# New task lists for a hand-scheduled recurrent-gate and soft-mixture kernel, with one small load moved to another queue

## Chip, cores and metric

One NeuronCore of a Trainium2 chip runs the whole kernel. The metric is the device time of one execution in microseconds (us), the median of several runs.

## What is computed

The reference, cut to what matters (float32 throughout, 4 sequences of 5056 tokens of 256 channels, 20224 tokens in all):

```python
# part 1: gated linear recurrence over time, for each channel
sig_r, sig_i = 1/(1+exp(-r_gate)), 1/(1+exp(-i_gate))
a_t  = exp(8 * sig_r * log(sigmoid(a_param)))
h    = a_t[:, t] * h + sqrt(1 - a_t[:, t]**2) * sig_i[:, t] * x[:, t]   # y[:, t] = h
# part 2: soft mixture of experts over all tokens y; phi is 256 x 32, 8 experts of 4 slots
logits = y @ phi
d = softmax(logits, over tokens);  slot_input = d.T @ y
slot_out = relu(slot_input[e] @ w1[e]) @ w2[e]          # 1024 hidden, for each expert e
out = softmax(logits, over slots) @ slot_out
```

## The kernel before

The tokens are cut into 40 blocks of 512 (the last has 256), called quads, and the quads into 22 units: unit 0 is quad 0, units 1 to 18 are pairs of quads, units 19 to 21 single ones. For each unit three loads come from HBM: `Dr` (the r gate, with channels on partitions), `Di` and `Dx` (the i gate and x, with tokens on partitions). A pair's load is 1 MiB. All of them go out on SyncE's queue; `w10` to `w27` are the 16 loads of expert weights, 1 MiB each, on the same queue (`w22` is the second matrix of expert 2).

What a unit goes through, with the names that the lists use (p is a unit, q a quad, h one of two halves of the channels, g a group of up to two units):

- ScalarE: `SRp` and `SIp` (a tanh each, lines 814 and 832), `EXp.h` (the exponential that makes a, line 888, for two units at once where they are paired), `RTp` (the square root, line 904). Exponential and tanh share one table of functions, the square root needs another, so roots are done in blocks between two table loads.
- `SQp.h` (a squared, line 873) on GpSimd or VectorE, now and then ScalarE.
- `Uq` (gated x) on VectorE or GpSimd. A string `IV` with one letter for each quad says how: D is one fused VectorE instruction (line 852); P is an addition of 1 on GpSimd (`P1q`, line 842) and a product (line 854); E is the product alone, and TensorE adds x to it by transposing two tiles into the same PSUM bank instead of one.
- TensorE: `TUp.h` (line 921) transposes gated x to channels on partitions, in PSUM. VectorE: `STp.h` (line 944) multiplies by the root, `SCp.h` (line 964) is the scan over time.
- `TYq` (line 987) transposes the result back, `YCq` (line 1001 or 1003) copies it out. `LGg`, `LEg`, `LDg`, `TEg`, `ESg`, `DMg`, `ACg`, `AEg` are the logits of a group (line 1047, reading `phi_sb`), their running maximum, and the softmax sum over tokens that is rescaled as it goes (`AE`, line 1135).

After the last unit comes a serial stretch: `W`, `SP`, `SL`, `SM` (merging four partial sums, lines 1327 to 1339), the expert layers `L1` and `L2`, and then the outputs: `CT`, `CM`, `CS`, `CE`, `RR`, `RC`, `CN` (softmax over slots), `OT` (line 1584), `OE` (lines 1599 and 1601) and the stores `OD` on SyncE's queue.

The order of work is not left to the hardware. `ORDER` has one list for each engine, written out task by task, and a list `B` in which the tasks that claim tiles from the shared pool `all_s` (48 slots of 512 KiB) must claim them. A planner in the same file (`Planner.run`) walks the lists with assumed durations to decide which slot each task gets, and emits the instructions in that order; each engine then runs its list from top to bottom, each instruction waiting for its inputs. The constants `XFER`, `LAG0` and the like are the planner's assumed transfer times; they act on the kernel through the slots that are given out.

Around the change: the kernel's constants are set up in `e_const` (which also starts the load of `a_param` on ScalarE's queue), `phi` is loaded on SyncE's queue right behind `Dx4` (line 756), and every logit task waits for that.

Of the kernel before, what the change touches and what calls it, by code (L numbers as in the profile page):

```python
# [15 lines left out]
P = 128  # L16
# [12 lines left out]
IV = 'DDDPEEEEDEEEEEEEEEEEEEEEEDDEEPEPPPPPPPPP'  # L29
# [42 lines left out]
PHI = 4  # L72
# [31 lines left out]
    ),  # L104
    "ACT": (
# [12 lines left out]
    ),  # L118
# [14 lines left out]
    ),  # L133
    "POOL": (
# [6 lines left out]
    ),  # L141
# [6 lines left out]
    ),  # L148
# [9 lines left out]
    ),  # L158
}
SWITCH = 0.09  # L160
WARMF = 1.4
COLD = 5.6
COLDX = 1.9
IDLE = 2.2
CHILL = 5.0
LOAD = 1.41

# [7 lines left out]
SI2 = ()  # L175
RT2 = ()
XFER = 1.265
ISSUE = 0.4
FIRST = 0.7
REACH = 2.6  # L180
REACHO = 1.55
LATO = 1.75
DEEP = 8
PEX = 1.03

ODS = 0

LAG1 = 0.8
LAG0 = 1.6

OUT2 = (4, 5, 6, 7, 8)

KIND = {
    "exp": ("exp", "ln"), "ln": ("ln",), "tanh": ("exp", "sig"), "sig": ("sig",), "sqrt": ("sqrt",),
}

class Task:
# [367 lines left out]
def kernel(  # L569
# [171 lines left out]
    def load(nm, p):  # L741
# [20 lines left out]
        if (nm, p) in (("r", 0), ("x", PHI)):  # L762
            ld[(nm, p)].parts = 2
# [935 lines left out]
```

## Time and profile before

| | |
|---|---|
| median of 3 runs | 285.18 us (285.14 to 285.29) |
| the profiled execution | 285.39 us |
| its span (first to last instruction on the core) | 283.6 us |
| granted TensorE clock, mean over the span | 0.994 |
| VectorE busy | 226.9 us of the span |
| ScalarE busy | 242.0 us |
| TensorE busy (identity transposes that fill gaps are counted) | 259.8 us |
| GpSimd busy | 184.8 us |
| moved by DMA | 100.07 MB |

An engine's busy time counts its instructions, not its waits for others; a VectorE or GpSimd instruction that is held up while it runs counts as busy. The span is what the timeline's zero and end refer to. The 1.8 us between the span and the execution's time lie outside the program's instructions.

### The profile page before, as it was taken

What the parts mean: (1) busy time and instruction counts of PE and PEld (TensorE: products, weight loads), DVE (VectorE), ACT (ScalarE), POOL (GpSimd) and SP (SyncE); (2) the same over time, 40 slices, a digit from 0 to 9 for tenths busy, and PEclk for the clock granted to TensorE, in tenths of its full rate; (3) what the DMA queues carried; (4) which work ended last, traced back from release to release, by engine and by line L of the source; (5) the groups of instructions that cost most, each with busy time, mean ns of one, the idle gap of its engine ahead of it and who ended that gap; (6) DMA issues with size and microseconds to landing.
All of it is one profiled execution on the core that took longest, in us unless ns stands there. A gap on an engine that the chain in (4) does not pass through costs nothing.

```text
span 283.6 us, 6612 instructions
## 1 busy us (share of the span) xinstructions
PE 259.8 (92%) x2760; PEld 208.2 (73%) x2760; DVE 226.9 (80%) x270; ACT 242.0 (85%) x247; POOL 184.8 (65%) x147
## 2 busy tenths in 40 slices
PE   7999798599989898898998899899999999999897
PEld 7999797469966676676677567565656677788796
DVE  0153999999999999998999989999974768758340
ACT  7898999999999999999999899999861279876620
POOL 4228769999999989996989999998110501211100
PEclk9999999989999999999999999999999999999999
DMA  7999999999999999995999998978850049999995
GB/s 229 422 425 424 419 416 419 424 422 417 422 419 381 383 407 415 424 387 202 419 374 391 344 410 316 340 249 317 326 232 2 2 192 414 418 424 421 423 416 226
DMA packets 14960, 100.07 MB, mean 353 GB/s; under 512 B 1745, under 2 KB 2002, under 8 KB 4306
## 3 DMA queue, kind: packets, MB, share of 16 engines
q1 hardware_dynamic: 14928, 99.65, 87.5%
q8 instruction: 21, 0.34, 0.5%
q14 instruction: 9, 0.07, 0.1%
q10 hardware_dynamic: 2, 0.00, 0.0%
HBM read 78.94 MB, written 20.71 MB: 351 GB/s over the span
## 4 chain that ended last, share of the span: by engine, by line
DVE 41%; PE 36%; DMA 11%; issue 7%; ACT 4%; POOLq 0%; SPq 0%; DVEq 0%; ACTq 0%
DVE all_s L964 19%; DVE pair L944 12%; DMA all_s<-in_i_gate_dram 8%; PE bank L1260 6%; PE bank L1584 5%; PE pair L921 4%; PE one L1260 3%; DVE yn L1003 3%; DMA all_s<-in_x_dram 3%; PE pair L987 3%; DVE all_s L852 2%; PE bank L1434 2%; PE bank L1382 2%; PE one L1047 2%; PE bank L1554 2%
## 5 line engine op out<-in xcount | busy, mean ns | idle before, releaser
L964 DVE TENSOR_TENSOR_SCAN all_s<-all_s,pair 128x1024 f32<-128x1024 f32 (+8 forms) x50 | 92.9, 1879 | 0.6
L854 POOL TENSOR_TENSOR all_s<-all_s 128x1024 f32<-128x1024 f32 (+1 forms) x34 | 79.9, 2370 | 6.9 <-ACT all_s L832 3.7
L873 POOL TENSOR_TENSOR all_s<-all_s 128x1024 f32<-128x1024 f32 (+2 forms) x40 | 70.7, 1795 | 17.6 <-ACT all_s L888 14.6
L921 PE MATMUL pair<-ident,all_s 128*128 128x128 f32 x480 | 59.0, 274 | 5.6 <-DVE all_s L964 4.0
L921 PEld LDWEIGHTS pair<-ident,all_s 128*128 128x128 f32 x480 | 52.6, 140 | 11.3 <-DVE all_s L964 4.4
L1260 PE MATMUL one<-ident 128*128 128x128 f32 x394 | 50.4, 282 | 0.5 <-DVE all_s L1061 0.5
L987 PE MATMUL pair<-ident,all_s 128*128 128x128 f32 x316 | 42.7, 280 | 7.3 <-DVE all_s L964 4.2
L1260 PEld LDWEIGHTS one<-ident 128*128 128x128 f32 x394 | 46.2, 146 | 1.5 <-DVE all_s L1061 0.7
L987 PEld LDWEIGHTS pair<-ident,all_s 128*128 128x128 f32 x316 | 34.9, 142 | 15.8 <-DVE all_s L964 6.4
L944 DVE SCALAR_TENSOR_TENSOR pair<-all_s,pair 128x1024 f32<-128x1024 f32 (+1 forms) x38 | 44.6, 1186 | 0.6 <-ACT all_s L904 0.2
L888 ACT ACTIVATE all_s<-all_s,ca 128x2048 f32<-128x2048 f32 (+3 forms) x28 | 43.9, 1589 | 0.1
L1531 POOL TENSOR_TENSOR all_s<-all_s,rs_all 128x512 f32<-128x512 f32 (+3 forms) x12 | 10.5, 897 | 48.8 <-DVE rs_all L1528 47.0
L832 ACT ACTIVATE all_s<-all_s 128x2048 f32<-128x2048 f32 (+2 forms) x22 | 38.1, 1731 | 2.2 <-DMA all_s<-in_i_gate_dram 2.2
L814 ACT ACTIVATE all_s<-all_s 128x2048 f32<-128x2048 f32 (+2 forms) x22 | 37.6, 1731 | 0.7 <-DMA all_s<-in_r_gate_dram 0.7
L904 ACT ACTIVATE all_s<-all_s 128x2048 f32<-128x2048 f32 (+2 forms) x22 | 37.2, 1733 | 0.1
L1001 ACT COPY yn<-pair 128x1024 f32<-128x1024 f32 (+1 forms) x25 | 24.4, 987 | 0.3 <-ACT yn L1001 0.3
L1047 PE MATMUL one<-all_s,phi_sb 128*32 128x256 f32 (+1 forms) x344 | 23.6, 382 | 0.5 <-DVE all_s L964 0.5
L1599 ACT COPY all_s<-bank 128x512 f32<-128x512 f32 (+1 forms) x38 | 20.0, 578 | 4.7 <-PE bank L1584 2.9
L1120 PE MATMUL one<-yn,eS 128*32 128x257 f32 x312 | 21.7, 386 | 2.4 <-ACT eS L1101 0.9
L1260 PE MATMUL bank<-ident 128*128 128x128 f32 x166 | 22.7, 275 | 0.8 <-ACT all_s L1599 0.7
L1601 DVE COPY all_s<-bank 128x512 f32<-128x512 f32 (+1 forms) x28 | 16.1, 604 | 6.8 <-PE one L1584 5.0
L1260 PEld LDWEIGHTS bank<-ident 128*128 128x128 f32 x166 | 18.6, 140 | 2.8 <-ACT all_s L1599 1.8
(115 smaller groups left out, 314.4 us busy)
## 6 DMA issues: line engine op xcount, KB each, us to landing
all_s<-in_r_gate_dram SPq DMA_DIRECT2D x18, 1024.0 KB, 10.8
all_s<-in_i_gate_dram SPq DMA_DIRECT2D x18, 1024.0 KB, 12.0
all_s<-in_x_dram SPq DMA_DIRECT2D x18, 1024.0 KB, 10.4
all_s<-in_moe_w_dram SPq DMA_DIRECT2D x16, 1024.0 KB, 7.6
out_dram<-all_s SPq DMA_DIRECT2D x5, 2048.0 KB, 9.8
out_dram<-all_s SPq DMA_DIRECT2D x8, 1024.0 KB, 6.7
all_s<-in_i_gate_dram SPq DMA_DIRECT2D x3, 512.0 KB, 4.4
all_s<-in_x_dram SPq DMA_DIRECT2D x3, 512.0 KB, 7.4
```

The source lines that it names most:

```text
L814: nc.scalar.activation(v, v, AF.Tanh, scale=0.5)
L832: nc.scalar.activation(v, v, AF.Tanh, scale=0.5)
L854: eng.tensor_tensor(out=o, in0=a, in1=b, op=ALU.mult)
L873: eng.tensor_tensor(out=t(Nb[(p, h)])[:, :c], in0=v, in1=v, op=ALU.mult)
L888: nc.scalar.activation(v, v, AF.Exp, scale=ca[:, h : h + 1], bias=ca[:, h : h + 1])
L904: nc.scalar.activation(v, v, AF.Sqrt, bias=f, scale=-f)
L921: nc.tensor.matmul(t(up)[:, i, m * P : (m + 1) * P], raw(nm, q)[:, m * D + h * P : m * D + (h + 1) * P], ident, is_transpose=True, start=( ...
L944: nc.vector.scalar_tensor_tensor(v, w, 1e-3 if gate_of(quads(p)[0]) == "S" else 0.5e-3, u, op0=ALU.max, op1=ALU.mult)
L964: nc.vector.tensor_tensor_scan(dst, dst, flat()[:, s0:s1], init, op0=ALU.mult, op1=ALU.add)
L987: nc.tensor.transpose(out=flat()[:, b * D + h * P : b * D + (h + 1) * P], in_=t(A[p])[:, h, i * QT + (b0 + b) * P : i * QT + (b0 + b + 1) ...
L1047: nc.tensor.matmul(o.rearrange("s (i p) -> s i p", p=P), phi_sb[:, h, :], t(A[p])[:, h, : plen(p)].rearrange("c (i j p) -> c j i p", j=nb, ...
L1260: nc.tensor.transpose(out=t(b)[:, 0, :P] if b.tag == "pair" else t(b)[:, :P], in_=ident, identity=ident)
```

## The change

Six things, all in one edit:

1. New lists in `ORDER`. VectorE's and ScalarE's tasks up to the merge differ in order, and four squares (`SQ0.0 SQ0.1 SQ1.0 SQ1.1`) go from GpSimd to VectorE, one (`SQ19.0`) from ScalarE to GpSimd. Loads and claims are in a new order. Among the tasks of the output stretch some 55 change between VectorE and ScalarE. `const2` (16 small copies on GpSimd) is put behind `U4`, `CE3` moves from the output stretch to a place ahead of `SR21`.
2. `IV`: quads 3, 29, 31 and 33 go from P to E, quads 28 and 30 from E to P.
3. `phi` is loaded from `e_const`, second on ScalarE's queue; it is gone from SyncE's queue, and the logits' tasks have no dependency on `Dx4` any more.
4. The planner takes 1.1 times the transfer time for loads of the first units.
5. `LAG0` is 0.1 instead of 1.6, for a first large load issued before 2.5 us.
6. `PHI` is gone, with what hung on it.

The heads of the lists (before, then after) and the rest of the diff:

```diff
-IV = 'DDDPEEEEDEEEEEEEEEEEEEEEEDDEEPEPPPPPPPPP'
+IV = 'DDDEEEEEDEEEEEEEEEEEEEEEEDDEPEPEPEPPPPPP'
-PHI = 4
     "DVE": (
-        "CA SQ3.1 U0 SQ3.0 SQ2.1 U1 U2 ST0.0 ST0.1 SC0.0 SC0.1 ST1.1 ST1.0 SC1.0 SC1.1 ST2.0 SC2.0 ST2.1 SC2.1 U8 YC0.0 "
+        "CA SQ0.0 SQ3.1 SQ0.1 SQ3.0 U0 SQ1.1 SQ2.1 SQ1.0 U1 U2 ST0.1 SC0.1 ST0.0 SC0.0 ST1.0 SC1.0 ST1.1 SC1.1 ST2.0 "
...
-        "SC20.1 LE9 LD9 LE10 ST21.1 LD10 SC21.1 ST21.0 SC21.0 MP AE9 LE11 LD11 MX AE10 W AE11 AF SL SM CM9 CS9 RR1 RR9 "
+        "SC20.0 SC19.1 ST20.1 AE8 SC20.1 LE9 ST21.1 LD9 LE10 LD10 SC21.1 ST21.0 SC21.0 MP AE9 LE11 LD11 MX W AE10 AE11 "
+        "AF CM10 SL CM9 SM RR3 CS10 CS9 RR1 RR9 CM5 HS0 CS5 RR10 RC3 RD HR0 CM0 RB1 CS0 RR5 RC9 RR0 RC0 HR1 SO RB5 RC10 "
     "ACT": (
-        "SA LN SI0 SR0 EX0.1 EX0.0 SR3 EX3.1 SR2 EX3.0 SR1 EX1.1 EX1.0 SI2 SI1 RT0.0 RT1.0 RT3.0 RT2.0 SI3 SR4 SR5 SI4 "
+        "SA LN SR0 SI0 EX0.1 EX0.0 SR3 EX3.1 EX3.0 SR2 SR1 EX1.1 EX1.0 SI1 SI2 RT0.0 RT1.0 RT3.0 RT2.0 SI3 SR4 SR5 SI4 "
     "PE": (
-        "CB TU0.0 TU0.1 TU1.1 TU1.0 TU2.0 TU2.1 TU3.1 LG0.0 LG0.1 LG0.2 TY0.0 TU3.0 LG1.0 TY2.0 TY1.0 TY3.0 LG1.1 LG0.3 "
+        "CB TU0.1 TU0.0 TU1.0 TU1.1 TU2.0 TU2.1 TY2.0 TU3.0 TY1.0 LG0.0 LG1.0 TY3.0 LG1.1 TU3.1 LG0.1 LG0.2 TU4.1 TY0.0 "
     "POOL": (
-        "const const2 SQ0.1 SQ0.0 SQ1.1 SQ1.0 SQ2.0 U4 P13 U3 U6 U5 U7 SQ5.0 SQ5.1 SQ4.0 SQ4.1 SQ6.0 SQ7.0 SQ7.1 U9 "
+        "const U3 SQ2.0 U4 const2 U6 U5 U7 SQ5.0 SQ4.1 SQ5.1 SQ4.0 SQ6.1 U9 SQ7.1 SQ7.0 SQ6.0 U10 U11 U12 LD0 U13 U14 "
     "SP": (
-        "Di0 Dr0 Dr3 Dr2 Dr1 Dx0 Di2 Dx1 Di1 Dx2 Dr4 Di3 Dr5 Dx3 Di4 Dx4 Dr7 Dr6 Di5 Di6 Dr9 Dx5 Dx6 Dr8 Di8 Dx7 Di7 "
-        "Dr11 Di9 Dx8 Dr10 Dr14 Dr15 Di10 Dx11 Dx9 Dr13 Dr12 Di11 Dx10 Di12 Dx12 w27 Di14 Dx14 Di13 Di16 w17 w13 Dx13 "
+        "Dr0 Di0 Dr3 Dr2 Dr1 Dx0 Di1 Di2 Dx1 Dx2 Dr5 Di3 Dr4 Dx3 Di4 Dx4 Dr7 Dr6 Di5 Dx5 Di6 Dx6 Di8 Dr9 Di7 Dr8 Dx7 Dx8 "
+        "Dr10 w22 Dr11 Di10 Di9 Di14 Dx9 Dx12 Dr12 Dx10 Dr13 Di11 Dx11 Di12 Di19 Dr14 Dr15 Dx14 Di13 w16 Di16 Dx13 Dx16 "
...
-LAG0 = 1.6
+LAG0 = 0.1
...
-                    landed[0] += LAG1 + (LAG0 if now < 1.9 else 0.0)
+                    landed[0] += LAG1 + (LAG0 if now < 2.5 else 0.0)
...
         nc.scalar.dma_start(out=row, in_=a_param.rearrange("(o c) -> o c", o=1))
+        nc.scalar.dma_start(out=phi_sb, in_=phi.rearrange("(p h) s -> p h s", p=P))
...
-            if (nm, p) == ("x", PHI):
-                nc.sync.dma_start(out=phi_sb, in_=phi.rearrange("(p h) s -> p h s", p=P))
...
-        ld[(nm, p)] = add("SP", f"D{nm}{p}", XFER * c / QT - (0.045 if c > QT else 0.5 if len(ld) == 0 else 0) + (0.27 if (nm, p) == ("x", PHI) else 0),
+        ld[(nm, p)] = add("SP", f"D{nm}{p}", XFER * c / QT * (1.1 if p < 4 - (nm != "r") else 1.0) - (0.045 if c > QT else 0.5 if len(ld) == 0 else 0),
...
-        if (nm, p) in (("r", 0), ("x", PHI)):
+        if (nm, p) == ("r", 0):
             ld[(nm, p)].parts = 2
...
-                         deps=[SC[(p, h2)] for h2 in range(h + 1)] + [ld[("x", PHI)]], gate=begun(lg),
+                         deps=[SC[(p, h2)] for h2 in range(h + 1)], gate=begun(lg),
```

## Rows read from the trace of the kernel before

**Rows 1.** The page: busy us (share of the span) xinstructions; DMA share, 40 slices, tenths.

```profile
PE 259.8 (92%) x2760; PEld 208.2 (73%) x2760; DVE 226.9 (80%) x270; ACT 242.0 (85%) x247; POOL 184.8 (65%) x147
...
DMA  7999999999999999995999998978850049999995
```

**Rows 2.** Windows: PE, PEld, DVE, ACT, POOL busy; PE clock, DMA share, GB/s.

```profile
20.00:30.00 10.00, 10.00 (x94) 10.00 (x93) 4.33 (x3) 8.79 (x6) 9.15 (x5) 1.00 1.01 422
30.00:40.00 10.00, 8.55 (x78) 8.17 (x77) 9.96 (x9) 9.97 (x7) 6.86 (x4) 1.00 1.02 417
...
150.00:160.00 10.00, 8.52 (x86) 6.99 (x79) 10.00 (x9) 9.01 (x11) 10.00 (x6) 1.00 0.96 376
160.00:170.00 10.00, 8.73 (x102) 5.74 (x103) 8.96 (x10) 9.95 (x8) 9.26 (x6) 1.00 0.97 392
```

**Rows 3.** Timeline of ScalarE: start, us, what [idle before it, and releaser].

```profile
24.18 1.92 ACT L832 ACTIVATE all_s<-all_s 128x2048 f32<-128x2048 f32 x1 [1.18 <-DMA all_s<-in_i_gate_dram]
26.11 1.28 ACT L904 ACT_TABLE_LOAD   x1
27.40 6.46 ACT L904 ACTIVATE all_s<-all_s 128x1024 f32<-128x1024 f32 x4
...
106.39 1.89 ACT L832 ACTIVATE all_s<-all_s 128x2048 f32<-128x2048 f32 x1
...
157.52 1.91 ACT L832 ACTIVATE all_s<-all_s 128x2048 f32<-128x2048 f32 x1 [0.99 <-DMA all_s<-in_i_gate_dram]
```

**Rows 4.** Timeline of VectorE, at the start and at the merge.

```profile
19.23 1.23 DVE L873 TENSOR_TENSOR all_s<-all_s 128x1024 f32<-128x1024 f32 x1 [1.51 <-ACT all_s L888]
26.12 4.55 DVE L852 SCALAR_TENSOR_TENSOR all_s<-all_s 128x1024 f32<-128x1024 f32 x2 [5.67 <-ACT all_s L832]
30.60 1.28 DVE L944 SCALAR_TENSOR_TENSOR pair<-all_s,pair 128x512 f32<-128x512 f32 x2
...
208.49 0.48 DVE L1135 SCALAR_TENSOR_TENSOR accS<-accS,dm,one 128x257 f32<-128x257 f32 x1
208.88 0.28 DVE L1327 TENSOR_SCALAR W<-R,wj 128x128 f32<-128x128 f32 x1
209.08 0.59 DVE L1135 SCALAR_TENSOR_TENSOR accS<-accS,dm,bank 64x128 f32<-64x128 f32 x2
210.24 0.19 DVE L1339 COPY yn<-bank 128x32 f32<-128x32 f32 x1 [0.57 <-PE bank L1332]
...
211.01 0.41 DVE L1508 TENSOR_REDUCE rm<-bank 128x8 f32<-128x256 f32 x1
```

**Rows 5.** Chain of work that ended last, in order of time: start, us, what.

```profile
5.12 19.04 DMA all_s<-in_i_gate_dram
...
27.27 3.41 DVE all_s L852
```

**Rows 6.** Timeline of GpSimd.

```profile
26.77 2.82 POOL L854 TENSOR_TENSOR all_s<-all_s 128x1024 f32<-128x1024 f32 x1 [0.85 <-DMA all_s<-in_x_dram]
...
59.50 2.39 POOL L854 TENSOR_TENSOR all_s<-all_s 128x1024 f32<-128x1024 f32 x1
61.84 1.90 POOL L873 TENSOR_TENSOR all_s<-all_s 128x1024 f32<-128x1024 f32 x1
```

**Rows 7.** Line 752, the issue at 4.14 us (`Di2`): its landing.

```profile
DMA to landing us min/median/max: 15.0/15.0/15.0
```

**Rows 8.** Line 752, the issue at 96.0 us (`Di12`): its landing.

```profile
DMA to landing us min/median/max: 8.9/8.9/8.9
```

**Rows 9.** Timeline of SyncE's queue: the first load of a weight.

```profile
100.85 0.33 SPq L1276 DMA_DIRECT2D all_s<-in_moe_w_dram  x1
```

**Rows 10.** Timeline of TensorE: eight transposes in a row; the merge.

```profile
165.27 1.09 PE L921 MATMUL pair<-ident,all_s 128*128 128x128 f32 x8
...
209.47 0.67 PE L1332 MATMUL bank<-W,accS 128*128 128x32 f32 x4
```

97 rows, old and new, of the table ORDER are left out of this document.

## Prediction

> **What bounds the kernel now.** I read the busy totals and the DMA digits of the page, then busy time in windows of 10 us, then each engine's timeline at the places that the new lists change, then the chain and the landings of single loads.
>
> The totals say that no engine is full over the span [rows 1]; the windows say otherwise. Between 30 and 200 us VectorE, ScalarE and, in most windows, GpSimd are busy almost without a gap, while DMA runs at its full 420 GB/s and more than 90% busy up to the eighteenth slice, some 127 us, and TensorE has little left later [rows 1, 2]. So work taken from one engine there is worth only what its neighbours can follow. The places where VectorE and ScalarE stand idle are few: the start, one wait of ScalarE late [rows 3], and the serial merge at the end [rows 4]. The reader is to see the start above all: from 20 to 30 us VectorE is busy 4.33 us of 10 [rows 2].
>
> What holds the start is a load. `Di1` is third from the end of the first ten loads and lands at 5.12 + 19.04 = 24.16 us [rows 5]; ScalarE waits 1.18 us for it [rows 3], `SI1` and then the table load and four roots follow, and VectorE, idle for 5.67 us, starts `U1` at 26.12 [rows 4]. A second thing goes wrong there: `U1` and `U2` take 4.55 us together where such an instruction otherwise takes 1.2 (the square on the same tile size) [rows 4]. The chain has 3.41 us of it in the second [rows 5], and GpSimd's product `U4` runs from 26.77 to 29.59 [rows 6]: `U2` gets through just after that.
>
> **The change, part by part.**
>
> *Order of the first loads, `SI1` ahead of `SI2`.* `Di1` changes places with `Di2`, which landed at 4.14 + 15.0 = 19.1 [rows 7]. `Di2` then lands some 21.6 (1 MiB at 422 GB/s is 2.5 us [rows 2]), and `Dx1` takes the place of 24.16. ScalarE, free at 24.18 - 1.18 = 23.0 after its first tanh, need not wait: both tanh are done at 24.9 instead of 26.1. Gain 1.2 us at the first root (26.2 instead of 27.40 [rows 3]). `Dr0` before `Di0` only swaps two half-size loads that both have to be there.
>
> Not all of it lasts. In GpSimd's new list `SQ2.0` is behind `U3`, which needs `Dx2`, there at 26.7 [rows 6]. A free product takes 2.39 and a square 1.90 [rows 6], so `SQ2.0` is done at 31.0 or 31.1; `RT2`, fourth of the block, would be due at 27.40 + 6.46 - 1.9 - 1.2 = 30.8 [rows 3]. ScalarE waits 0.3. Term: **-0.9** (from -1.2 to 0, the latter if an input comes just in time a little later).
>
> *VectorE's start.* `U1` can begin when `Dx1` lands, 24.2; GpSimd is then idle until 26.7, so the two take 1.2 each and end at 26.6. `ST0` waits for the first root, 27.3, where before it began at 30.60 [rows 4]: 3.3 us sooner. The four squares that VectorE takes over (a 1024-column one is 1.23 [rows 4]) fall into its idle time before 24 us; GpSimd loses work that it did while nothing waited. But VectorE cannot stay 3 us ahead of ScalarE, which delivers every a and root and is full from 30 to 150. What the surplus can do is take away ScalarE's remaining waits, through slots that come free sooner. The one to see is 0.99 us for `Di18` at 157.52 [rows 3], a load that now also stands one MiB earlier in the list. Term: **-0.8** (from -1.0 to 0). If VectorE's lead counted in full and nothing else, it would be -3.1: the far end.
>
> *phi on ScalarE's queue.* It is 32 KiB, which at 422 GB/s is under 0.1 us of all engines, and no wait of the trace before names it; the issue stands in ScalarE's idle time before its first activation. Term 0, either way.
>
> *Squares and exponentials moved.* `SQ19.0` leaves ScalarE, `CE3` comes to it ahead of its last units: one 128x512 operation each, they cancel. `const2` sits in GpSimd's list where it waited for `SI3` anyway. The planner's constants and `IV` for quad 3 act at a time when TensorE fills its time with identity transposes. Term 0.
>
> *`IV` late.* Quads 29, 31 and 33 to E, 28 and 30 to P: one more E quad net, eight transposes of 1.09 us together [rows 10], in a stretch in which TensorE has 1.3 to 1.5 us of each 10 left [rows 2]. It is hidden by those gaps unless the scan is waiting for just this transpose. Term **+0.3** (from 0 to +1.1), nearer the hidden end because both windows have more room than 1.09.
>
> *The merge.* VectorE's list has `W AE10 AE11 AF CM10 SL CM9 SM` for `AE10 W AE11 AF SL SM`. `W` waits for an exponential until 208.88, and `AE10` (0.48), which used that wait, now comes behind it [rows 4]; `SP` on TensorE (209.47 [rows 10]) needs `AE11`, so it moves by up to 0.4. `CM10` (0.41 [rows 4]) stands ahead of `SL`, which had 0.57 of waiting in front of it [rows 4], so most of that is hidden. `SL` and `SM` start `L1`, and from there to the first store all is serial. Term **+0.45** (from 0 to +0.9, both in full).
>
> *One weight early.* `w22` goes from the 67th MiB to the 29th. It takes 2.5 us of DMA and two of the 48 slots from some 70 us on, where the first weight used to come at 100.85 [rows 9]. Loads with long lead (`Dr14`, `Dr15`, `Dr11`) are pushed back for it, those with short lead are not: `Di10` is 2 MiB sooner. Term 0; if the cover is gone, up to +2.5.
>
> Sum: -0.9 - 0.8 + 0.3 + 0.45 = -0.95. Against the profiled execution, 285.39 (span 283.6, 1.8 outside), that is 284.44. It stood 0.21 above the median of the runs, so the forecast is **284.2**, from 282.6 to 284.6 in its own case: the far end of VectorE's lead, 285.18 - 3.1 + 0.45, and the line of 0.2%, 0.57 us, below which a measurement of this kernel can't well tell a gain from no change.
>
> **Rivals.**
>
> *The start is given back (no change).* Two ways. First, inputs just in time: `Di12` landed at 96.0 + 8.9 = 104.9 and was used at 106.39 [rows 3, 8], a lead of 1.5, and up to some 127 us DMA is full [rows 1], so an engine that is ahead meets loads that are not. ScalarE's 0.9 and the late wait shrink to 0.5 or so; with +0.75 for late `IV` and merge that is 285.4. Against it: most of the loads with a short lead were moved up.
>
> Second, the port. If `Dx1` lands later than 25.5, `U2` starts after GpSimd's `U3` at 26.7 and waits for it: 26.7 + 2.39 + 1.2 = 30.3, and VectorE's start is the old one [rows 4, 6]. The point is a slip of 1.3 us. VectorE then has no surplus, the -0.8 is gone, and the time is 285.18 - 0.9 + 0.75 = 285.0. [...]
>
> *Slots run short (slower).* `w22` holds its two slots, a quarter of what one unit occupies, through the stretch in which leads are 1.5 us [rows 3, 8]. From the point at which a load that ScalarE needs comes 1.5 us later than now, it decides: the full 2.5 us would leave ScalarE waiting 1.0, with the start's 1.7 unused and +0.75 from the end, so 286.9. For it: DMA has no reserve there [rows 1]. Against it: later weights come later than before, and up to 100 us only this one stands there.
>
> *The merge is worse (slower).* `HR1` now stands behind a row of reductions and reciprocals while `L2` runs; if `L2` waits for it by 0.5 and both +0.9 and the late +1.1 come true, with ScalarE's 0.9 kept and no more: 285.18 - 0.9 + 2.5 = 286.8; with half of these 286.0.
>
> **How the numbers follow.** Forecast 0.50; the start given back 0.25 (0.15 by arrival, 0.10 by the port); slots 0.14; merge 0.11. The forecast's case lies beyond 0.57 us below 285.18; the given-back cases lie within it; the last two above. So faster 0.50, same 0.25, slower 0.25. The range from 282.4 to 286.5 leaves out the far end of VectorE's lead with more recovered elsewhere (some 0.06) and the worse half of the slower cases (some 0.12).
>
> **What would show it.** Right: `SI1` without a wait before it, the first root near 26.2, `U1` and `U2` at 1.2 each and ended by 26.7, `ST0` near 27.4; the end of the four roots near 33.0 instead of 33.86; no wait of about 1 us for a load near 155; `SL`, the last step ahead of `L1`, 1.0 us or more sooner than 210.24 [rows 4]. Wrong: a VectorE product of 3 us near 26; a wait of ScalarE for `RT2`'s square of more than 0.5; DMA share under 1 between 60 and 100 us with ScalarE waiting for a load; `SL` more than 0.6 further behind `AF` than now; VectorE waiting for a transpose of unit 16 or 17.

## The result: slower, 287.50 us, and the profile after

The changed kernel takes 287.50 us (median of 7 runs, 286.54 to 289.01), the kernel before 285.29 beside it (7 runs, 285.05 to 286.16): a ratio of 1.0085, 95% interval 1.0056 to 1.0114. I had forecast 284.2, a gain, and a range up to 286.5. The profiled execution, the fastest of its runs, took 286.54; its span is 284.5 us, against 283.6. Ratios here and below compare the means of the runs, without single ones over 1.5% above the fastest of their kernel; times in us are medians of all runs.

This fastest execution has 1.15 us of the 2.2 by which the medians differ, and next to nothing of that ahead of the merge. `W`, in the merge, starts at 208.94 us in it, against 208.88 before; `SL` is 0.65 us later than before, the end of the span 0.9, and 0.25 of the 1.15 us lie outside the span.

ScalarE's start before, which [rows 3] does not have:

```profile
4.86 1.06 ACT L832 ACTIVATE all_s<-all_s 128x1024 f32<-128x1024 f32 x1
...
9.13 1.92 ACT L814 ACTIVATE all_s<-all_s 128x2048 f32<-128x2048 f32 x1 [0.68 <-DMA all_s<-in_r_gate_dram]
```

ScalarE's timeline after, to be read beside these lines and [rows 3]:

```profile
8.13 1.06 ACT L830 ACTIVATE all_s<-all_s 128x1024 f32<-128x1024 f32 x1 [1.47 <-DMA all_s<-in_i_gate_dram]
...
10.60 1.91 ACT L812 ACTIVATE all_s<-all_s 128x2048 f32<-128x2048 f32 x1
...
22.55 3.70 ACT L830 ACTIVATE all_s<-all_s 128x2048 f32<-128x2048 f32 x2
26.28 1.28 ACT L902 ACT_TABLE_LOAD   x1
27.57 6.46 ACT L902 ACTIVATE all_s<-all_s 128x1024 f32<-128x1024 f32 x4
...
155.00 1.91 ACT L830 ACTIVATE all_s<-all_s 128x2048 f32<-128x2048 f32 x1 [0.94 <-DMA all_s<-in_i_gate_dram]
```

`SI1` (22.55) has no wait before it, as I forecast, and still the first root starts at 27.57, later than the 27.40 of before. The loss is ahead of it: `SI0` waits 1.47 us for the half load `Di0`, and `SR3`, the first full tanh, starts at 10.60; in the kernel before it started at 9.13, and `SI0` at 4.86. The late wait for an i gate has not gone either: 0.94 now, 0.99 before.

VectorE, at the start and at the merge, beside [rows 4]:

```profile
24.48 2.36 DVE L850 SCALAR_TENSOR_TENSOR all_s<-all_s 128x1024 f32<-128x1024 f32 x2 [0.30 <-ACT all_s L830]
28.66 0.70 DVE L942 SCALAR_TENSOR_TENSOR pair<-all_s,pair 128x512 f32<-128x512 f32 x1 [1.82 <-ACT all_s L902]
...
208.94 0.29 DVE L1325 TENSOR_SCALAR W<-R,wj 128x128 f32<-128x128 f32 x1 [0.36 <-ACT wj L1324]
209.14 0.48 DVE L1133 SCALAR_TENSOR_TENSOR accS<-accS,dm,one 128x257 f32<-128x257 f32 x1
209.72 0.60 DVE L1133 SCALAR_TENSOR_TENSOR accS<-accS,dm,bank 64x128 f32<-64x128 f32 x2
210.25 0.41 DVE L1506 TENSOR_REDUCE rm<-bank 128x8 f32<-128x256 f32 x1
210.89 0.19 DVE L1337 COPY yn<-bank 128x32 f32<-128x32 f32 x1 [0.23 <-PE bank L1330]
```

`U1` and `U2` take 2.36 us together instead of 4.55, and `ST0` comes 1.9 us sooner. VectorE then stands waiting for roots; its view of waits after says so (total us, times, longest):

```profile
DVE pair L942 <- ACT all_s L902: 5.6, 5, 1.8
```

In the merge `W` starts at the same time as before, 208.9, `AE10` and `CM10` follow where they delay, and `SL` comes at 210.89 instead of 210.24.

What I had not looked for stands on TensorE. The clock line of the page (40 slices, tenths of full speed), then TensorE's timeline, then its windows (busy, clock, DMA share, GB/s), all of after:

```profile
PEclk9999999999999979999999999999999999999999
```

```profile
99.00 1.09 PE L985 MATMUL pair<-ident,all_s 128*128 128x128 f32 x8 [1.88 <-DVE all_s L962]
101.33 3.22 PE L919 MATMUL pair<-ident,all_s 128*128 128x128 f32 x16 [1.24 <-POOL all_s L852]
```

```profile
96.00:100.00 4.00, 2.12 (x22) 1.00 1.01 422
100.00:104.00 4.00, 2.76 (x16) 0.72 1.01 424
104.00:108.00 4.00, 4.00 (x35) 0.85 0.69 279
```

TensorE idles 1.88 us before `TY8`, 1.24 before `TU9`, and then its granted clock is 0.50 in each window of 1 us from 102 to 105 us, and 1.00 before 101 and after 106 (0.72 and 0.85 are means over windows that hold part of that). `TU9`'s 16 transposes take 3.22 us, and VectorE waits for them:

```profile
104.66 1.23 DVE L942 SCALAR_TENSOR_TENSOR pair<-all_s,pair 128x1024 f32<-128x1024 f32 x1 [1.23 <-PE pair L919]
```

The kernel before has such a stretch too, at 56 to 59 us (its window, then the one wait of over 1 us that TensorE has in it near 100 us):

```profile
56.00:59.00 3.00, 3.00 (x27) 0.50 1.02 423
```

```profile
99.73 1.09 PE L987 MATMUL pair<-ident,all_s 128*128 128x128 f32 x8 [1.34 <-DVE all_s L964]
```

### The profile page after: what moved, and what is told of

Read it like the earlier page. It is cut to its first block, busy times and chain, and to the rows that moved or that the text cites. A ratio compares the mean times of both kernels' runs of the same rounds, so it can differ in the third digit from the quotient of the medians.

```text
span 284.5 us, 6653 instructions
## 1 busy us (share of the span) xinstructions
PE 263.2 (93%) x2784; PEld 212.2 (75%) x2784; DVE 230.1 (81%) x279; ACT 239.1 (84%) x241; POOL 175.3 (62%) x142
## 4 chain that ended last, share of the span: by engine, by line
ACT 36%; PE 29%; DVE 16%; DMA 8%; POOL 5%; issue 5%; SPq 0%; DVEq 0%; ACTq 0%; POOLq 0%
DVE all_s L962 9%; ACT all_s L830 8%; ACT all_s L886 8%; ACT all_s L812 7%; ACT all_s L902 7%; PE bank L1258 6%; PE bank L1582 6%; DVE pair L942 5%; DMA all_s<-in_i_gate_dram 4%; DMA all_s<-in_x_dram 3%; POOL all_s L871 3%; PE pair L919 2%; PE bank L1432 2%; PE one L1258 2%; POOL all_s L852 2%
## 5 line engine op out<-in xcount | busy, mean ns | idle before, releaser
L871 POOL TENSOR_TENSOR all_s<-all_s 128x1024 f32<-128x1024 f32 (+2 forms) x37 | 64.3, 1765 | 7.7 <-ACT all_s L886 4.4
L919 PE MATMUL pair<-ident,all_s 128*128 128x128 f32 x496 | 62.3, 278 | 4.0 <-DVE all_s L962 1.7
L919 PEld LDWEIGHTS pair<-ident,all_s 128*128 128x128 f32 x496 | 55.4, 142 | 10.3 <-issue 3.3
L985 PE MATMUL pair<-ident,all_s 128*128 128x128 f32 x316 | 42.4, 279 | 7.1 <-DVE all_s L962 4.2
L985 PEld LDWEIGHTS pair<-ident,all_s 128*128 128x128 f32 x316 | 35.0, 142 | 16.6 <-DVE all_s L962 6.2
L1258 PEld LDWEIGHTS one<-ident 128*128 128x128 f32 x376 | 44.8, 147 | 1.9 <-issue 0.7
L1045 PE MATMUL one<-all_s,phi_sb 128*32 128x256 f32 (+1 forms) x344 | 22.8, 368 | 0.6 <-DVE all_s L962 0.6
L1597 ACT COPY all_s<-bank 128x512 f32<-128x512 f32 (+1 forms) x35 | 18.4, 563 | 3.4 <-PE bank L1582 2.8
L1599 DVE COPY all_s<-bank 128x512 f32<-128x512 f32 (+1 forms) x31 | 18.3, 617 | 3.2 <-PE bank L1582 2.2
L1582 PE MATMUL bank<-all_s,lD 32*128 32x256 f32 x216 | 19.5, 396 | 0.0
```

The lines of the kernel that those rows point to most:

```text
L871: eng.tensor_tensor(out=t(Nb[(p, h)])[:, :c], in0=v, in1=v, op=ALU.mult)
L919: nc.tensor.matmul(t(up)[:, i, m * P : (m + 1) * P], raw(nm, q)[:, m * D + h * P : m * D + (h + 1) * P], ident, is_transpose=True, start=( ...
L985: nc.tensor.transpose(out=flat()[:, b * D + h * P : b * D + (h + 1) * P], in_=t(A[p])[:, h, i * QT + (b0 + b) * P : i * QT + (b0 + b + 1) ...
L1258: nc.tensor.transpose(out=t(b)[:, 0, :P] if b.tag == "pair" else t(b)[:, :P], in_=ident, identity=ident)
L1582: nc.tensor.matmul(t(op)[:, k * D : (k + 1) * D], t(hT)[r, (k0 + k) * P : (k0 + k + 1) * P], t(soRb)[r, :D], start=True, stop=True)
```

## Experiments

Times are medians; "before" is the kernel before on the same chip. Beside these runs it took 285.11 to 285.49 us, so a difference of a few tenths between two experiments says little. Theories: **A**, `Dr0` ahead of `Di0` delays the third load and eats the gain of the start; **B**, the merge order; **C**, TensorE's lower clock near 100 us; **D**, late loads (`Di13`, `Di18`) that an earlier ScalarE meets.

### The start

**e3_i_first**, the changed kernel with the first two loads turned round again:

```diff
 SP, B: -Dr0 Di0 Dr3   +Di0 Dr0 Dr3
 ACT:   -SR0 SI0 EX0.1 +SI0 SR0 EX0.1
```

> The changed kernel with Di0 before Dr0 in the loads and the claims and SI0 before SR0 on ScalarE, as before; phi stays first. Theory A with the order as cause: Di0 lands near 4.2 instead of 8.1, SR3 starts near 9.2, the median is 1.0 to 1.5 below 287.5. With phi as cause: Di0 sooner, but SR3 near 10.5, and at most 0.3 gained. Theory B: nothing gained.

287.13 us (ratio to before 1.0066, 1.0042 to 1.0089). ScalarE:

```profile
8.72 1.92 ACT L811 ACTIVATE all_s<-all_s 128x2048 f32<-128x2048 f32 x1 [0.28 <-DMA all_s<-in_r_gate_dram]
...
25.69 4.67 ACT L901 ACTIVATE all_s<-all_s 128x1024 f32<-128x1024 f32 x3
...
155.25 1.92 ACT L829 ACTIVATE all_s<-all_s 128x2048 f32<-128x2048 f32 x1 [1.62 <-DMA all_s<-in_i_gate_dram]
```

`SR3` is 1.9 us sooner and so is the first root: A holds for the start. But the lead is gone at the root of unit 16 (165.6 us; 165.3 in the changed kernel): 0.53 us into a wait for `Di13`, 1.62 into one for `Di18`, and TensorE's lower clock stands at 100 us here too (0.58 from 100 to 104). Of the 1.88 us at the first root, 0.97 are left at the root of unit 12 (130.42; 131.39 in the changed kernel), so most of the loss comes behind it. The median gains 0.37.

**e11_r_first** is the reverse, the kernel before with only this pair turned (`+Dr0 Di0`, `+SR0 SI0`).

> The kernel before with only Dr0 ahead of Di0 and SR0 ahead of SI0. If this order is what delays the third load, SR3 starts near 10.5 us instead of 9.1; the wait of 1.18 us before SI1 takes up most of that, so the first root starts at 27.4 to 27.8 us and the time is 0 to 0.4 us more. If the delay in the changed kernel came from something else in its start, SR3 stays at 9.1 us and the time is the same.

286.07 us (1.0032, 1.0004 to 1.0060).

```profile
10.42 1.92 ACT L813 ACTIVATE all_s<-all_s 128x2048 f32<-128x2048 f32 x1
...
25.64 1.92 ACT L831 ACTIVATE all_s<-all_s 128x2048 f32<-128x2048 f32 x1 [1.38 <-DMA all_s<-in_i_gate_dram]
...
28.87 4.67 ACT L903 ACTIVATE all_s<-all_s 128x1024 f32<-128x1024 f32 x3
```

`SR3` is late as expected. My expectation that `SI1`'s wait would absorb it was wrong: all following loads are late as well, the wait is still 1.38, and the whole 1.5 us reaches the first root. The time is 0.78 us more, not 0 to 0.4; the profile is of a slower execution than the median, 287.55.

**e1_phi_back** (the changed kernel, `phi` back on SyncE's queue behind `Dx4`) and **e2_phi_only** (the kernel before, `phi` second on ScalarE's queue) ask whether `phi` is what delays the start.

```diff
 e_const:  -nc.scalar.dma_start(out=phi_sb, ...)          (e1; e2 adds it)
 load Dx4: +nc.sync.dma_start(out=phi_sb, ...)            (e1; e2 removes it)
```

> The changed kernel with phi back on SyncE's queue behind Dx4, all lists as changed. Theory A (the start: the front of the loads lands 1.5 us later, ScalarE is full from there to 200 us and passes it on), with phi as its cause: SR3 starts near 9.2 us instead of 10.6, the first root near 26.2 instead of 27.6, and the median is 1.0 to 1.5 below the changed kernel's 287.5. Theory A with the order Dr0 before Di0 as cause: SR3 stays at 10.6 and the median at 287.5. Theory B (the loss is in the merge and later): no change either.

> The kernel before, with nothing changed but phi, which is loaded second on ScalarE's queue. Theory A with phi as cause: SR3 starts 1 to 1.5 us later than 9.1 and the median is 286.3 to 286.8. Theory A with the order of the first two loads as cause, or theory B: 285.1 to 285.5, SR3 at 9.1.

e1: 288.18 us (1.0088, 1.0062 to 1.0114), `SR3` at 10.5. e2: 284.94 us (0.9986, 0.9975 to 0.9997), `SR3` at 9.0. `phi` is not the cause; by itself its move is a small gain.

The profile of e1 bears on theory C. Its lists are those of the changed kernel, but in this execution (288.63 us) the clock is lower for longer (0.55 from 100 to 104 us and 0.59 from 104 to 108; 0.72 and 0.85 in the changed kernel): the root of unit 8 is at 92.29 (92.39 in the changed kernel), that of unit 12 at 132.61 (131.39), that of unit 16 at 167.41 (165.29).

### TensorE's clock, the merge, the weights

**e5_keep_busy**: the changed kernel with the transposes `TY7` issued three times and `TY8` twice, 24 more of them, which add work to TensorE and change no result.

```diff
-for b in range(nb):
+for b in [*range(nb)] * {7: 3, 8: 2}.get(q, 1):
```

> The changed kernel; the transposes of TY7 are made three times and those of TY8 twice, into the same place (24 more of 0.14 us, 3.3 us), where TensorE stands idle for 1.9 and 1.2 us between 97 and 102 us. Theory C (TensorE's clock falls to half just there, for 3.4 us or more, and what waits for it passes the loss on: over the runs so far each 0.006 less of mean clock goes with some 1.1 us): the mean clock is 0.999 or 1.0 in most runs, the median 285.9 to 286.5. Theory D (the loads of the second half come too late in the new order, the clock only goes along): the clock is up, but the median stays at 287.2 or above.

286.15 us (1.0027, 1.0006 to 1.0048), 1.35 below the changed kernel (1.7 by the ratios, whose intervals do not meet); the mean granted clock was 0.999 or 1.0 in all 12 runs, 0.982 to 0.994 in the 7 of the changed kernel. TensorE's timeline and window, and VectorE's line behind `TU9`:

```profile
101.42 1.94 PE L918 MATMUL pair<-ident,all_s 128*128 128x128 f32 x16 [0.36 <-POOL all_s L851]
```

```profile
100.00:104.00 4.00, 3.63 (x34) 1.00 1.02 426
```

```profile
103.47 1.23 DVE L941 SCALAR_TENSOR_TENSOR pair<-all_s,pair 128x1024 f32<-128x1024 f32 x1
```

More work on TensorE makes the kernel faster: `TU9` takes 1.94 instead of 3.22, and VectorE goes on 1.19 us sooner. C holds, by the medians of 12 and 7 runs. In the two profiled executions little of it is left at the end: the last scan starts at 204.81 here, at 204.98 in the changed kernel, whose profile is of its fastest run.

**e4_merge_back**: the changed kernel with the old order of the merge.

```diff
 DVE: -MX W AE10 AE11 AF CM10 SL CM9 SM  +MX AE10 W AE11 AF SL SM CM10 CM9
 ACT: -ES11 DM11 WE DM10 HZ              +DM11 ES11 DM10 WE HZ
```

> The changed kernel with VectorE's merge in the old order (AE10 before W; CM10 and CM9 behind SM) and ScalarE's exponentials there in the old order. Theory B (the merge order costs 0.6 us, as the profile's SL and SM show): SL 0.4 to 0.6 sooner after AF's inputs, the median 286.9. Theory A: the same 0.6 at most, and the rest of the loss stays. If neither the start nor the merge accounts for more than half of the 2.2 us, the loss is somewhere in the middle.

287.75 us (1.0057, 1.0028 to 1.0086). From the last scan's start to `AF` it is 4.5 us; 5.0 in the changed kernel, 4.4 before. So B is real and 0.5 to 0.6, but no median shows it, since these runs spread with the clock: 284.91 to 287.58 in the five with a mean of 0.999 or 1.0; with 0.988, 287.46 to 288.32 in four and 289.70 in a fifth.

In its profiled execution the mean granted clock is 1.0, and TensorE has the same two waits ahead of `TY8` and `TU9`:

```profile
99.62 1.09 PE L984 MATMUL pair<-ident,all_s 128*128 128x128 f32 x8 [1.89 <-DVE all_s L961]
101.95 1.94 PE L918 MATMUL pair<-ident,all_s 128*128 128x128 f32 x16 [1.24 <-POOL all_s L851]
```

So the fall does not come each time that these waits do. This run took 287.58 us all the same, with 2.16 us of waiting for `Di18`; late loads, theory D, can cost time without the clock, and how much stays open.

**e6_weights_behind**: the changed kernel with `w26` and `w10` behind `Di17` in the lists SP and B, no longer ahead of `Di18`.

```diff
-w25 Dr17 w26 Dx15 w10 Di18 Dr19 Di17   +w25 Dr17 Dx15 Di18 Dr19 Di17 w26 w10
```

> The changed kernel with the weights w26 and w10, which stand between Dr17 and Di18 in the loads and claims, put behind Di17. Theory D: SI18 no longer waits 0.9 to 2.2 us for its load, and the median is 1.0 to 1.5 below 287.5. Theory C: that wait shrinks, but TensorE's clock still falls near 100 us in most runs and no more than 0.7 is gained.

287.36 us (1.0060, 1.0027 to 1.0093). The wait for `Di18` is gone; waits of 1.53 for `Di13` and 0.65 for `Dr15` stand in its place. The mean granted clock is below 0.999 in 7 of the 9 runs, 0.987 in the profiled one, where VectorE waits 1.65 us for `TU9` (1.23 in the changed kernel): as theory C had it. D as I put it (these two weights) explains no loss by itself.

**e8_all** undoes all four (e3, e4, e5, e6 in one); **e9_three** leaves the weights where the change put them.

> The changed kernel with Di0 first, the old merge order, w26 and w10 behind Di17, and TensorE kept busy between 97 and 102 us, all four. If the start (1.2 to 1.5), the merge (0.5), the clock (1 to 2) and the late loads (1) add up on ScalarE's path: 283.8 to 284.6, faster than before. If the four overlap (the late loads take back whatever ScalarE gains): 285.3 to 286.

> The changed kernel with Di0 first, the merge's old order and the repeated transposes, but with the weights w26 and w10 left ahead of Di18; against the one with the weights moved too, which took 284.99 us. If the place of the weights costs time of its own, ScalarE waits again for Di18 before SI18, 0.3 to 2 us as in the runs of the changed kernel's list, and the time is 285.5 to 286.3 us. If it costs nothing once the clock is held and the start is mended, SI18 has no more than 0.2 us of wait or the time is within 0.3 us of 285.0.

e8: 284.99 us (0.9979, 0.9957 to 1.0000). e9: 285.04 us (0.9992, 0.9973 to 1.0011), with a wait of 1.16 us for `Di18` in its profile. e8 lies between my two cases. The place of the weights is worth nothing that shows; start order, clock and merge together are worth 287.50 - 285.04 = 2.46 us. Singly they gave 0.37, 1.35 and nothing by the medians, 0.5, 1.7 and 0.8 by the ratios; only the clock's is clear of the spread, so whether the three hide each other's gains or simply add up is not shown.

### What the start alone is worth

**e10_start_only**: the kernel before with `phi` on ScalarE's queue and only this of the new lists:

```diff
 SP:  -Di2 Dx1 Di1 Dx2  +Di1 Di2 Dx1 Dx2
 ACT: -SI2 SI1 RT0.0    +SI1 SI2 RT0.0
```

**e12_vector_start** is e10 with four squares moved to VectorE:

```diff
 DVE:  -CA SQ3.1 U0 SQ3.0 SQ2.1 U1 U2          +CA SQ0.1 SQ0.0 SQ3.1 SQ3.0 U0 SQ1.1 SQ2.1 SQ1.0 U1 U2
 POOL: -const2 SQ0.1 SQ0.0 SQ1.1 SQ1.0 SQ2.0   +const2 SQ2.0
```

> The kernel before with phi second on ScalarE's queue and, of the new lists, only Di1 ahead of Di2 and SI1 ahead of SI2. If my forecast's step of the start was right in itself and failed in the changed kernel only by the r gate's half load ahead of Di0, SR3 starts near 9.0 us, SI1 has no wait before it, the first root starts near 26.2 us, and the time is 0.5 to 1.2 us less than that of the kernel before. If loads further on arrive just in time anyway, the first root starts near 26.2 us too, but ScalarE waits for an i gate at units 12 to 18, the root of unit 16 comes at 164.7 us or later, and the time is within 0.4 us of the kernel before.

> The kernel with only Di1 first, SI1 first and phi on ScalarE's queue (284.82 us), and besides four squares (SQ0.0, SQ0.1, SQ1.0, SQ1.1) moved from GpSimd to VectorE as in the changed kernel. In the run without them the products U1 and U2 took 5.99 us together beside three squares of GpSimd. If VectorE's start is worth something, as my forecast had it at 0.8, the products take 2.4 us, the first scan starts 2 to 3 us sooner and the time is 284.0 us or less. If VectorE's lead is worth nothing because ScalarE delivers the roots and is full, the first scan starts sooner too, VectorE waits for roots further on, the root of unit 16 stays at 163.3 us, and the time is 284.6 to 285.1.

e10: 284.82 us (0.9984, 0.9967 to 1.0001). e12: 284.93 us (0.9986, 0.9960 to 1.0011). VectorE and ScalarE of e10, then of e12:

```profile
24.09 5.99 DVE L850 SCALAR_TENSOR_TENSOR all_s<-all_s 128x1024 f32<-128x1024 f32 x2 [3.91 <-DMA all_s<-in_x_dram]
...
25.82 6.46 ACT L902 ACTIVATE all_s<-all_s 128x1024 f32<-128x1024 f32 x4
```

```profile
24.31 2.35 DVE L850 SCALAR_TENSOR_TENSOR all_s<-all_s 128x1024 f32<-128x1024 f32 x2
27.16 1.29 DVE L942 SCALAR_TENSOR_TENSOR pair<-all_s,pair 128x512 f32<-128x512 f32 x2 [0.50 <-ACT all_s L902]
...
157.27 1.92 ACT L830 ACTIVATE all_s<-all_s 128x2048 f32<-128x2048 f32 x1 [0.91 <-DMA all_s<-in_i_gate_dram]
```

In e10 the first root is at 25.82, 1.6 us sooner than before, and ScalarE keeps 1.6 to the root of unit 16 (163.3) and 1.0 to the last scan; yet the median is 0.47 below before, and `phi` alone (e2) was 0.55 below its own before. That is neither of the two cases that I had written down. In e12 `ST0` is 2.8 us sooner than in e10 (30.00 there), and the time is the same: VectorE's lead is worth nothing that shows. The root of unit 16 came at 164.64, not at 163.3 as expected, and the wait for `Di18` that the lead was to take away is 0.91 (0.04 in e10); but TensorE's mean granted clock is 0.994 in the profile of e12 and 1.0 in that of e10, its fastest run, so these two figures do not compare the lists alone.

### The early weight

**e7_w22_late** is the changed kernel with `w22` moved from behind `Dr10` to behind `w27`, in SP and B. **e13_w22_late_clear** puts VectorE's `U26 U25` behind `CM3 CS3` besides. **e14_w22_early** is the kernel before with `w22` behind `Dr10`, nothing else.

```diff
 e7, e13, SP and B: -Dr10 w22 Dr11    +Dr10 Dr11 ... w27 w22 Dx20
 e13, DVE:          -AE2 U26 U25 CM3 CS3  +AE2 CM3 CS3 U26 U25
 e14, SP and B:     -w15 w22 w24      +w15 w24 ... and Dr10 w22 Dr14
```

> The changed kernel with the weight w22, which the new lists load as the 29th MiB, put behind w27 (the 67th) in loads and claims. The forecast's rival 'slots run short': the loads from 75 us on come 2.5 us sooner and the median falls by 1 us or more. Theories C and D: ScalarE did not wait for a load between 60 and 100 us, so nothing is gained there; the median stays within 0.5 of 287.5.

> The changed kernel with w22 late, as in the run that took 292.01 us, and with VectorE's U26 and U25 put behind CM3 and CS3. In that run the two products took 10.80 us instead of 2.35 while GpSimd did five squares without a gap, and CM3, which stood behind them, kept TensorE and ScalarE waiting 6.8 us. If that meeting on the port is the whole loss, the wait of 6.8 us is gone and the time is 286 to 288 us, that of the changed kernel or 1 us less. If the late load of w22 itself costs it, the time stays above 290 us.

> The kernel before with only the load of w22 moved from the 67th MiB to behind Dr10, where the changed kernel has it. If the early weight is covered, as the forecast had it, ScalarE waits for no more loads than before and the time is that of the kernel before within 0.4 us. If slots and transfers run short by it, every load behind it comes up to 2.5 us later, ScalarE waits for an r or i gate between 90 and 160 us, and the time is 286 to 288 us.

e7: 292.01 us (1.0216, 1.0174 to 1.0258). The profile is of its slowest run, 295.58; the five others have a median of 290.98. VectorE, GpSimd and ScalarE of the profiled run:

```profile
126.16 10.80 DVE L849 SCALAR_TENSOR_TENSOR all_s<-all_s 128x1024 f32<-128x1024 f32 x2
...
124.51 9.31 POOL L870 TENSOR_TENSOR all_s<-all_s 128x1024 f32<-128x1024 f32 x5
...
141.43 1.01 ACT L998 COPY yn<-pair 128x1024 f32<-128x1024 f32 x1 [6.83 <-PE pair L984]
```

Two products that take 2.35 us in the changed kernel take 10.80 beside five squares that GpSimd issues without a gap; `CM3` and `CS3` are queued behind them, TensorE behind `CS3`, ScalarE behind TensorE. In the changed kernel GpSimd happens to stand still for 1.72 us just there, and the products pass. The load itself is not priced by this run.

e13: 296.80 us (1.0398, 1.0371 to 1.0424). The meeting was not taken away: the products took 5.86 us, the first 2.5 of them beside the squares, and `CM3`, now first, waited 3.07 for TensorE. By what I had written, over 290 blames the late load. The trace has something for that: from 130 to 150 us loading nearly stops, here and in e7 (DMA share 0.45 and 0.37 there; 0.89 and 0.99 in the changed kernel), while SyncE's queue waits for slots: in e13 7.8 us, until the two products are done, then 8.7 for a `TY` on TensorE. Windows of e13 (columns as for e14 below):

```profile
130.00:140.00 10.00, 6.84 (x74) 4.38 (x72) 8.95 (x6) 9.99 (x8) 10.00 (x7) 1.00 0.46 144
140.00:150.00 10.00, 7.22 (x56) 5.32 (x57) 9.38 (x8) 3.67 (x4) 4.05 (x3) 0.66 0.37 134
```

So the held-up products and the stopped loads hang together, and what the late weight costs by itself these two runs do not show.

e14: 298.57 us (1.0448, 1.0401 to 1.0495). Windows (PE, PEld, DVE, ACT, POOL busy; clock, DMA share, GB/s):

```profile
120.00:130.00 10.00, 7.59 (x72) 6.67 (x68) 8.79 (x8) 7.17 (x6) 7.20 (x5) 1.00 0.53 221
130.00:140.00 10.00, 7.10 (x68) 6.01 (x69) 3.33 (x5) 8.97 (x8) 3.96 (x3) 1.00 0.43 159
```

One weight some 36 MiB early costs 13.4 us in the old lists, and not by its transfer: DMA is half idle for 20 us, with its queue waiting for slots, up to 13.6 us at a time, and VectorE is busy 3.33 of 10 from 130 to 140. My reading: the slots are dealt out in a fixed order; two of them held longer stop the loads, and these the engines that would free the next. In the changed kernel the same early weight meets lists that were made for it, and between 60 and 100 us ScalarE waits for no load.

## Why the prediction was wrong

**The step that failed** is in "Order of the first loads": "`Dr0` before `Di0` only swaps two half-size loads that both have to be there". Turning them round costs 1.5 us at `SR3` and at the first root (e11 in the old lists; 1.9 come back in e3), which is all of the 1.2 that I had counted. The term was -0.9; in the profile it is +0.2 at the first root. In the whole time the step is worth less: 0.78 us in e11, 0.37 in e3. Why `Di0` lands at 8.1 us instead of 4.1 I can't settle: it is issued 0.9 us later, so most of the delay comes after the issue.

**The term was too large as well.** Where the start does gain 1.6 us (e10), hardly more than `phi`'s own gain reaches the median. The profile's -1.0 at the end of e10 is one execution, the fastest of its 12.

**VectorE's surplus, -0.8, is worth nothing.** The mechanism came true, with 2.36 instead of 4.55 and an earlier scan; the use that I gave it did not. VectorE waits for roots (5.6 us in five waits), and with nothing but the surplus added (e12) the time is that of e10 and the wait for `Di18` is 0.91. I had argued that VectorE "cannot stay 3 us ahead" and then given the surplus a price all the same; it should have been 0, with -0.8 as the far end.

**The term that was missing**, and the largest, is TensorE's clock, put at nothing: 1.35 us (e5). I had taken TensorE as "has little left" and its gaps as room to hide work in; the gaps are what this part of the loss comes from. In the profile of before, the stretch at half clock (0.50) lies where VectorE does not wait for TensorE, at 56 us; the new order has two waits, 1.88 and 1.24 us, ahead of transposes that VectorE's scan needs, where the old one had one of 1.34. In the runs the idle time and the lower clock go together: with the idle time filled (e5) the mean clock was 0.999 or 1.0 in all 12 runs and the 16 transposes took 1.94 us instead of 3.22; without that the mean clock was below 0.999 in 32 of the 40 runs of the changed kernel, e1, e3, e4 and e6, so not in all. What lowers the clock is not shown.

**Right:** the merge (+0.45 forecast; `SL` 0.65 later, 0.5 to 0.6 by the distance from the last scan); `phi` near 0; the port rival, which did not occur at 26 us (`U1` and `U2` took 2.36). Products held up did occur elsewhere: in e7 two of VectorE's lasted 10.80 us instead of 2.35, beside a row of five GpSimd squares. "The port" is only a name, in the forecast and in what I expected of e13: the runs show that two such products took longer beside GpSimd's work (4.55 us before, 5.99 in e10), not what holds them up. That `U2` would wait out the whole of `U3` (26.7 + 2.39 + 1.2) no run shows; it was my estimate, from the 3.41 us of `U2` beside `U4`. **Slots:** the rival's place was right as a danger, its price (2.5 us) far too low when the lists do not fit (13.4), and in the changed kernel it did not occur. Late `IV` (+0.3) was not tried by itself.

**The sum.** From the forecast 284.2 to 287.50 there are 3.3 us. 2.46 come back with the start order, the clock and the merge mended (e9). In e9 the merge is the old one, so what I had forecast for the rest is -0.9 - 0.8 + 0.3 = -1.4; measured is 285.04 - 285.29 = -0.25. The 1.15 missing is about the 0.8 of VectorE's surplus and 0.4 of the start, of whose 0.9 e10 shows 0.47 with `phi`'s own gain in it. This last is arithmetic on medians, not a run.

Two slips in the working: `Di1` is second, not third, from the end of the first ten loads, and 285.18 - 3.1 + 0.45 is 282.5, not 282.6. Nothing hangs on either.

No version clearly beats the kernel before: e10 (0.9984) and e8 (0.9979) have intervals that end at 1.000, and e2, `phi` alone, has the only one below it (0.9975 to 0.9997).

## What to carry to other kernels

Before a new order is priced, ask of each engine not only whether it is full but whether the new waits make it idle just ahead of work that others need: here 16 transposes behind two idle gaps of TensorE took 3.22 us instead of 1.94. Give an engine's lead a value only if the engine that bounds the stretch can use it. A hand-made order with a fixed deal of buffers is one object: one load moved alone cost some 4 us in one direction and 13.4 in the other, so such an entry can't be priced, or tried, without its list.

## What the runs showed that I had not expected

- Extra transposes that only keep TensorE busy made the kernel 1.35 us faster.
- Beside five GpSimd squares without a gap, two VectorE products that take 2.35 us in the changed kernel took 10.80 in one execution.
- A half-size load moved from first to second place, issued 0.9 us later, landed 4 us later (8.1 against 4.1 us).
- In the kernel before, runs with a mean granted clock of 0.994 and of 1.0 take the same time (285.04 and 285.07, 12 and 11 runs), but the three of 0.988 beside them have a median of 286.85; with the changed list and the old merge order (e4) the medians are 285.95 for 0.999 or 1.0 and 288.31 for 0.988.
